# A first chunk from three batches in a chunked mLSTM with two dense blocks

## The chip, the cores and the metric

The kernel runs on one core of a Trainium2 chip. The metric is the device time of one execution in microseconds, as the median of several runs. The core's engines are TensorE (PE; weight loads are PEld), VectorE (DVE), ScalarE (ACT), GpSimd (POOL) and SyncE (SP), which issues the DMA transfers here.

## The reference, cut to what matters

An mLSTM over 4 batches, 8 heads, 768 positions and head width 40, then two dense blocks on its 3072 tokens of width 320.

```python
for t in range(S):                      # per batch and head
    m_new = max(f[t] + m, i[t])
    C = exp(f[t] + m - m_new) * C + exp(i[t] - m_new) * outer(v[t], k[t])
    n = exp(f[t] + m - m_new) * n + exp(i[t] - m_new) * k[t]
    y[t] = sigmoid(o[t]) * (C @ q[t]) / max(abs(n @ q[t]), 1)
h = x @ w_in                            # 320 -> 2048
x2 = (max(h, 0) + alpha * min(h, 0)) @ w_out
out = max(x2 @ w1, x2 @ w2, x2 @ w3) @ w4   # 320 -> 768 -> 320
```

## The kernel before

The 3072 tokens are 24 tiles of 128 positions, six to a batch, and 8 chunks of three tiles (`CHUNKS`, L35). Tile number i is position i // 6 of the batches and i % 6 within one, called (batch, place) here.

Attention handles a tile at a time. Within it a score matrix is made per head (q and k), multiplied by decays (`db`), and multiplied with v; the earlier tiles of the batch come in through the carried state `C`. So a tile that is not the first of its batch also has an inter step (q on C), and one that is not the last a state step (k and weighted v, added to C). In TensorE's queue the score matmuls read `q`, the pov matmuls `va,db`, the state matmuls `vw,kv`, the inter matmuls `C,q`. Tiles of batch 0 go through `attention32` (L855) in float32. The others go through `attention` (L928): q, k, v and the score matrix are split into two 16-bit parts under scales of their batch (`batch_scale`, L746). There the matmuls read `qs,ks`, `vh,ph` and `cs,qs`, and the split q and k go through a staging tile `hl` that `qk_parts` (L915) fills for three tiles at once. `finish` (L842) divides, applies the output gate, splits the row for 16-bit matmuls, and transposes it into `xT`, by TensorE for the first three tiles (`BY_DMA`), by DMA after.

The first dense block works on a chunk: 16 units `m1_unit` (L1052) of 8 matmuls on `wi`, then `m2_tile` on `wo`. The second follows `LAG` = 4 chunks later with `m3_unit` on `wq` and `m4_tile` on `wp`. These four groups are the backbone of TensorE's work. The weights come as 64-bit floats; `f64_to_f32` and `conv` turn them into two 16-bit parts under a scale from norms that TensorE computes (matmuls on `cv`, `qs`, `ks`, borrowed as buffers for the conversion). `w_in` needs a last common factor, for which VectorE makes `dg` and TensorE multiplies it (`dg,ones`).

`gates` (L1290) makes all gate terms in two pieces of positions: the first `GSPLIT` = 2 tiles of each batch, and the rest. Decays go to memory (`ddr`) and come back spread over the partitions (`decays`, L790).

The order of instructions on every engine is not that of the program text. `Sched` records each operation, estimates its cost, and a list planner decides the order, and for some operations the engine. Where it expects TensorE to be idle early, it puts in fills, matmuls of ones that go nowhere (L569). So a changed dependency or buffer changes the order everywhere. Almost every instruction has line L574, where the planned operations are issued. Buffers are rings (`Ring`, L613): `q` has one buffer (L673), `db` two (L678), and a ring may borrow others through `more`.

Of the kernel before, what the change touches and what calls it, by code (L numbers as in the profile page):

```python
# [22 lines left out]
CT = S // 128  # L23
# [13 lines left out]
NMAX = max(CHUNKS) * 128  # L37
GSPLIT = 2

# [91 lines left out]
class Sched:  # L131
# [429 lines left out]
    def issue(self, order):  # L561
        lead = int(self.LEAD / 213)
        for i in order:
            op = self.ops[i]
            e = self.engines[op.eng]
            if op.eng == "pe":
                k, n = self.fill.get(i, (0, 0))
                for _ in range(k + lead):
                    e.matmul(  # L569
                        out=self.tiles[n][:, 0:256], lhsT=self.warmth[:, 0:128], rhs=self.warmth, start=True, stop=True  # L570
                    )
                lead = 0
            for meth, kw in op.calls:
                getattr(e, meth)(**{k: v.on(v.bank.tile) if isinstance(v, View) else v for k, v in kw.items()})  # L574
# [11 lines left out]
def kernel(  # L586
# [44 lines left out]
    id16 = sbt("id16", [128, 128], F16)  # L631
    ones_ = sbt("ones", [128, 256], BF16)
    ones = ones_[:, 0:128]
    sc.warmth = ones_
    al = sbt("al", [128, KF])
# [64 lines left out]

    r_cv.more = [t.rearrange("p h t -> p (h t)").bitcast(I32) for t in r_qs.t + r_ks.t]


# [80 lines left out]
    def sigmoids(g):  # L784
        t = r_sig()
        sp.dma_start(out=t, in_=tok[3 * g:3 * g + 3, :, 3, :].rearrange("c p d -> p c d"))
        act.activation(out=t, in_=t, func=ACTF.Sigmoid)
        sig_t[g] = t
# [28 lines left out]

    def state(c, kv, vw, gm):

        pcv = half(bank("a"))  # L820
        sc.unit()
        for h in range(4):
            for hh in range(2):
                k = 4 * hh + h

                pe.matmul(
                    out=pcv[64 * hh:64 * hh + 64, h], lhsT=kv[:, 0, k * D:k * D + 64], rhs=vw[:, k], start=True, stop=True
                )
        sc.end()
        if c == 0:  # L830
            cn = carry["C"] = r_c()
            copy(cn, pcv)
        else:
            cn = carry["C"]
# [6 lines left out]

    def finish(i, num, least, xt, t0):  # L842

# [7 lines left out]
        dve.tensor_tensor(out=y, in0=num[:, :, 0:D], in1=bc(dn, [128, H, D]), op=ALU.mult)  # L851
        combine(y, y, sig_t[i // 3][:, i % 3].rearrange("p (h d) -> p h d", d=D), ALU.mult)
        to_xT(split_x(y.rearrange("p h d -> p (h d)"), rx[:, i:i + 1]), xt, t0, i >= BY_DMA)

    def attention32(i, xt, t0):  # L855

        b, c = divmod(i, CT)
        last = c == CT - 1
        if i % 3 == 0:
            sigmoids(i // 3)  # L860
        t = r_q()
# [20 lines left out]
        if c:  # L882
            cn = carry["C"]
            for hh in range(2):
# [12 lines left out]
        if not last:  # L897
            vw = r_vw()
            combine(vw, va, bc(gt[2].unsqueeze(2), [128, H, VA]), ALU.mult)
            state(c, kv, vw, gm)  # L900
        pov = per_head(bank("a"))
# [9 lines left out]
        else:  # L911
            copy(num, pov)
        finish(i, num, 1.0, xt, t0)

    def qk_parts(i):  # L915

        x = scl[:, i // CT]
        for s in range(2):
            t, hl = r_q(), r_hl()
            for u in range(3):  # L920
                sp.dma_start(out=t[40 * u:40 * u + 40], in_=qk[i + u, s])
            for hh in range(2):
                sl = slice(4 * hh, 4 * hh + 4)
                scaled(hl[0:120, 0, sl], t[0:120, sl], x[0:120, 3 + s:4 + s])
                rest(hl[0:120, 1, sl], t[0:120, sl], x[0:120, 3 + s:4 + s], hl[0:120, 0, sl])
            carry[s] = hl

    def attention(i, xt, t0):  # L928

        b, c = divmod(i, CT)  # L930
        last = c == CT - 1
        x = scl[:, b]
        if i % 3 == 0:
            sigmoids(i // 3)
            qk_parts(i)
        gt, db, gm = decays(i)
        qs, ks = r_qs(), r_ks()
        u = 40 * (i % 3)
        for dst, hl, parts in ((qs, carry[0], (0, 0, 1)), (ks, carry[1], (0, 1, 0))):
# [23 lines left out]
        num = r_num()  # L963
        if c:
            cs = carry["cs"]
            piv = per_head(bank("a"))
# [8 lines left out]
        if not last:  # L975
            vw = r_vw()
            combine(vw[:, :, 0:D], v, bc(gt[2].unsqueeze(2), [128, H, D]), ALU.mult)
            dve.tensor_scalar(out=vw[:, :, D], in0=gt[2], scalar1=x[:, 10:11], scalar2=None, op0=ALU.mult)
            cn = state(c, kv, vw, gm)
            cp = r_cp()  # L980
            scaled(cp[:, 0], cn, x[:, 9:10])
            rest(cp[:, 1], cn, x[:, 9:10], cp[:, 0])
            cs = carry["cs"] = r_cs()
            for hh in range(2):
                sp.dma_start(
                    out=cpd[i, :, :, 4 * hh:4 * hh + 4].rearrange("a d h v -> d a (h v)"),
                    in_=cp[64 * hh:64 * hh + 40].rearrange("p a h v -> p a (h v)"),
                )
            sp.dma_start(out=cs[0:80], in_=cpd[i].rearrange("a d h v -> (a d) h v"))
            sp.dma_start(out=cs[80:120], in_=cpd[i, 0])  # L990

        pov = per_head(bank("a"))
        sc.unit()
        for h in range(H):
            for n, (a, e) in enumerate(((0, 0), (0, 1), (1, 0))):
                pe.matmul(out=pov[:, h], lhsT=ph[:, a, h], rhs=vh[:, e, h], start=(n == 0), stop=(n == 2))
        sc.end()
# [5 lines left out]
        else:  # L1003
            copy(num, pov)
        finish(i, num, x[:, 7:8], xt, t0)

# [91 lines left out]
    def m3_unit(j, f):  # L1098
# [18 lines left out]
        combine(h2_t[:, f, 1, 0:n], v, h2_t[:, f, 0, 0:n], ALU.subtract)  # L1117

    def m4_tile(j, t):
        i = ROW0[j] + t  # L1120
# [12 lines left out]
        iv = r_iv()  # L1133
        if i % CT == 0:
            dve.tensor_tensor(out=scl[:, i // CT, 8:9], in0=scl[:, i // CT, 2:3], in1=kw, op=ALU.mult)
        dve.scalar_tensor_tensor(
            out=iv, in0=rx[:, i:i + 1], scalar=scl[:, i // CT, 8:9], in1=rx2[:, i:i + 1], op0=ALU.mult, op1=ALU.mult
        )
        ob = r_ob()
        scaled(ob, ps, iv)  # L1140
        sp.dma_start(out=out[i * 128:(i + 1) * 128, :], in_=ob)

# [147 lines left out]
    def gates():  # L1290
# [11 lines left out]
        for c0, c1 in ((0, GSPLIT), (GSPLIT, CT)):  # L1302
# [12 lines left out]
            )  # L1315
            for b in range(B):
                sp.dma_start(
# [31 lines left out]
    def attend(j):  # L1349
        for t in range(CHUNKS[j]):  # L1350
            i = ROW0[j] + t
            (attention if i >= CT else attention32)(i, xT[j % 2], 128 * t)
            b, c = divmod(i, CT)
            if c == 1 and 0 < b < B - 1:
# [36 lines left out]
    with tc.manual_schedule():  # L1391
        make_identity(nc, ident)
        nc.vector.tensor_copy(out=id16, in_=ident)
        nc.vector.memset(ones_, 1.0)
        for t in r_va.t:
# [67 lines left out]
```

## Time and profile before

| | |
|---|---|
| median of 3 runs | 720.55 us (719.22 to 721.73) |
| span of the profiled execution | 717.8 us |
| that execution's own time around the span | not given by the page |
| TensorE busy | 685.9 us, 96% |
| VectorE, ScalarE, GpSimd busy | 484.9, 415.8, 159.4 us |
| mean granted TensorE clock | 0.950 of 2.4 GHz |

The span goes from the first to the last instruction. Busy time of TensorE in the profile counts a matmul from its modelled start to its end, whatever share of the array it uses. A granted clock of 1.00 is 2.4 GHz, 0.50 is 1.2 GHz.

### The profile page before, as it was taken

How to read it: one execution, taken by the hardware profiler on the slowest of the kernel's cores; microseconds unless marked ns; L12 is line 12 of the kernel's file. 1: busy time of each engine (PE TensorE's matmuls, PEld its weight loads, DVE VectorE, ACT ScalarE, POOL GpSimd, SP SyncE). 2: the span in 40 equal slices, each digit the busy share in tenths (PEclk: the TensorE clock that was granted, in tenths of full speed). 3: DMA queues.
4: the chain of work that ended last, by engine and by line, in shares of the span. 5: the costliest groups of instructions: out<-in, count | busy, mean ns of one | idle time of the engine just before them, and what ended most of it. 6: DMA issues, size and time to landing. Idle time of an engine off the chain costs nothing.

```text
span 717.8 us, 14674 instructions
## 1 busy us (share of the span) xinstructions
PE 685.9 (96%) x5299; PEld 464.1 (65%) x5299; DVE 484.9 (68%) x1256; ACT 415.8 (58%) x983; POOL 159.4 (22%) x193
## 2 busy tenths in 40 slices
PE   4789999999899999999999999999999999999998
PEld 3678766666566666666666666666766676666665
DVE  7676879999799899899579963786265223242332
ACT  4667769899799889887467662662253122222222
POOL 1221242044251362166014310330031000000000
PEclk8555799999999999999999999999999999999999
DMA  8865476565794656863443362122201110002000
GB/s 251 280 189 188 154 225 190 165 194 161 230 292 123 203 168 182 244 190 92 104 137 119 122 136 88 45 64 38 59 19 33 28 50 12 28 1 61 8 21 27
DMA packets 82802, 88.33 MB, mean 123 GB/s; under 512 B 38754, under 2 KB 66218, under 8 KB 82730
## 3 DMA queue, kind: packets, MB, share of 16 engines
q1 hardware_dynamic: 82730, 87.40, 42.2%
q8 instruction: 41, 0.67, 0.4%
q14 instruction: 31, 0.25, 0.1%
HBM read 60.83 MB, written 8.75 MB: 97 GB/s over the span
## 4 chain that ended last, share of the span: by engine, by line
PE 59%; DVE 2%; issue 0%; DMA 0%; SPq 0%; ACT 0%; ACTq 0%
PE bank L574 59%; DMA cs<-cpd 0%; SPq L574 0%; DVE wq L574 0%; DVE h L574 0%; DVE hl L574 0%; DVE vw L574 0%; DVE g L574 0%; DVE cp L574 0%; ACT db L574 0%; DVE y L574 0%; DVE gf L574 0%; DVE xs L574 0%; DVE cv L574 0%; ACT ob L574 0%
## 5 line engine op out<-in xcount | busy, mean ns | idle before, releaser
L574 PE MATMUL bank<-xT,wi 128*128 128x384 f16 x1024 | 177.1, 328 | 0.2 <-DVE gf L574 0.2
L574 PE MATMUL bank<-wo,g 128*128 128x320 f16 x1152 | 165.3, 299 | 0.6 <-DVE g L574 0.6
L574 PEld LDWEIGHTS <-wq 128*128 128x128 f16 x1152 | 110.9, 98 | 71.2 <-issue 0.5
L574 PEld LDWEIGHTS <-g 128*128 128x128 f16 x1152 | 110.9, 98 | 44.8 <-DVE g L574 0.9
L574 PEld LDWEIGHTS <-wi 128*128 128x128 f16 x1024 | 98.8, 98 | 62.3 <-issue 2.0
L574 PE MATMUL bank<-x2T,wq 128*128 128x384 f16 x720 | 123.1, 326 | 0.4 <-DVE gf L574 0.4
L574 POOL TENSOR_TENSOR g<-gf,g 128x384 f16<-128x384 f32 x63 | 60.6, 964 | 174.1 <-DVE g L574 95.3
L574 DVE TENSOR_TENSOR mv<-bank,mv 128x384 f32<-128x384 f32 x96 | 52.9, 551 | 60.4 <-PE bank L574 59.5
L574 DVE SCALAR_TENSOR_TENSOR gf<-d,al,bank 128x384 f32<-128x384 f32 x128 | 76.5, 603 | 9.9 <-ACT d L574 9.1
L574 ACT ACTIVATE h<-mv 128x384 f16<-128x384 f32 x47 | 24.5, 521 | 94.1 <-DVE mv L574 94.1
L574 ACT ACTIVATE d<-bank 128x384 f32<-128x384 f32 x128 | 61.1, 479 | 20.1 <-PE bank L574 18.8
L574 PE MATMUL bank<-xT,wq 128*128 128x384 f16 x432 | 70.7, 326 | 0.0
L574 ACT ACTIVATE db<-db,gtok 128x128 f32<-128x128 f32 x192 | 63.4, 390 | 9.1 <-POOL db L574 8.9
L574 ACT ACTIVATE g<-gf 128x384 f16<-128x384 f32 x104 | 53.7, 519 | 20.0 <-DVE gf L574 19.7
L574 PE MATMUL bank<-wp,h 128*128 128x320 f16 x432 | 61.0, 299 | 0.0
L574 PEld LDWEIGHTS <-h 128*128 128x128 f16 x432 | 42.1, 98 | 16.7
L574 POOL TENSOR_TENSOR h<-mv,h 128x384 f16<-128x384 f32 x14 | 13.8, 983 | 161.1 <-ACT h L574 161.0
L574 DVE TENSOR_TENSOR g<-gf,g 128x384 f16<-128x384 f32 x65 | 39.2, 610 | 11.3 <-ACT g L574 11.1
L574 POOL TENSOR_SCALAR_AFFINE_SELECT db<-db 128x512 f32<-128x512 f32 x48 | 36.7, 784 | 40.5 <-ACT gm L574 25.8
L574 DVE TENSOR_TENSOR db<-bank,db 128x512 f32<-128x512 f32 x48 | 31.8, 682 | 7.3 <-PE bank L574 2.0
L574 DVE TENSOR_SCALAR sx<-sx 128x1 int32<-128x1 int32 x48 | 7.0, 146 | 40.5 <-ACT xs L574 40.2
L574 ACT ACTIVATE xs<-bank 128x320 f16<-128x320 f32 x24 | 10.3, 429 | 37.1 <-PE bank L574 36.5
(170 smaller groups left out, 890.3 us busy)
## 6 DMA issues: line engine op xcount, KB each, us to landing
db<-ddr SPq DMA_DIRECT2D x24, 512.0 KB
raw<-tok SPq DMA_DIRECT2D x18, 480.0 KB
kv<-tok SPq DMA_DIRECT2D x24, 320.0 KB
q<-qk SPq DMA_DIRECT2D x36, 160.0 KB
raw<-w_out SPq DMA_DIRECT2D x16, 320.0 KB
raw<-w SPq DMA_DIRECT2D x9, 512.0 KB
qs<-hl SPq DMA_DIRECT2D x54, 80.0 KB
ks<-hl SPq DMA_DIRECT2D x54, 80.0 KB
```

What stands on the lines that cost most here:

```text
L574: getattr(e, meth)(**{k: v.on(v.bank.tile) if isinstance(v, View) else v for k, v in kw.items()})
```

## The change

The first chunk is now the first tile of batches 0, 1 and 2. After it come the remaining tiles in batch order: (0,1) to (0,5), (1,1) to (1,5), (2,1) to (2,5), then all six of batch 3 (`ORDER`). The three tiles of the first chunk and those of batch 0 go through `attention32` (`whole`), so eight tiles are float32, before six. The states of batches 1 and 2 that this leaves are kept (a second `C` buffer, and a borrowed `wp` buffer for batch 1) and split into 16-bit parts only when the second tile of the batch is reached (`state_parts`). `qk_parts` takes two tiles at once for places 1 and 2 of batches 1 and 2 (`GROUPS`). The gates are first made for 128 positions of each batch, then for 640. For the first tiles `q` borrows the `ph` buffer and one `hl` buffer, and `db` the other `hl`. The ones tile for fills is half as wide, and the fill reads it twice. The diff, cut:

```diff
-GSPLIT = 2
+GSPLIT = 1
+ORDER = [(b, 0) for b in range(B - 1)] + [(b, c) for b in range(B) for c in range(b < B - 1, CT)]
+GROUPS = {(b, c): n for b in range(B) for c, n in (((1, 2), (3, 3)) if b < B - 1 else ((0, 3), (3, 3)))}
+def whole(p):
+    b, c = ORDER[p]
+    return b == 0 or (c == 0 and b < B - 1)
...
-                        out=self.tiles[n][:, 0:256], lhsT=self.warmth[:, 0:128], rhs=self.warmth, start=True, stop=True
+                        out=self.tiles[n][:, 0:256].rearrange("p (a k) -> p a k", a=2), lhsT=self.warmth,
+                        rhs=self.warmth.unsqueeze(1).to_broadcast([128, 2, 128]), start=True, stop=True,
...
-    r_c = Ring("C", 1, [128, 4, VA])
+    r_c = Ring("C", 2, [128, 4, VA])
...
         if c == 0:
-            cn = carry["C"] = r_c()
+            cn = wp_s[KF2][:, 0:4 * VA].rearrange("p (h v) -> p h v", v=VA) if b == 1 else r_c()
+            carry["C", b] = cn
...
-    def qk_parts(i):
-        x = scl[:, i // CT]
+    def qk_parts(i, n):
+        x, r = scl[:, i // CT], slice(0, 40 * n)
...
+            if c == 1 and b < B - 1:
+                cn = carry["C", b]
+                dve.tensor_scalar(
+                    out=cn[:, :, D], in0=cn[:, :, D], scalar1=x[:, 10:11], scalar2=None, op0=ALU.mult
+                )
+                state_parts(i - 1, cn, x)
...
-            for b in range(B):
+            if c1 == 1:
+                sp.dma_start(out=ddr[0].rearrange("b c (h t) -> (b c h) t", t=128), in_=delta[:, t])
+            for b in range(B if c1 > 1 else 0):
...
             i = ROW0[j] + t
-            (attention if i >= CT else attention32)(i, xT[j % 2], 128 * t)
-            b, c = divmod(i, CT)
+            if i == 0:
+                r_q.more = [as_q(r_ph.t[0]), as_q(r_hl.t[0])]
+                r_db.more = [as_q(r_hl.t[1])]
+            elif i == 3:
+                r_q.more, r_db.more = r_q.more[:1], []
+            elif i == 8:
+                r_q.more = []
+            (attention32 if whole(i) else attention)(i, xT[j % 2], 128 * t)
+            b, c = ORDER[i]
```

The planner makes new orders from this. Three places follow; `ph` and `hl` in a score or inter matmul are borrowed q buffers, `hl` also a borrowed decay buffer. On TensorE, from the matmul on `dg` on, there stood before the inter step of the third tile, its pov and its state:

```order
L574 MATMUL bank_69<-dg_190,ones 128x4
L574 MATMUL bank_68<-C_168,q_149 128x41 x4
L574 MATMUL bank_64<-C_168,q_149 128x41 x4
L574 MATMUL bank_65<-va_161,db_158 128x41 x8
L574 MATMUL bank_67<-vw_164,kv_156 64x41 x8
```

and now the score step of the fourth tile (two banks in turn, four each) and the pov of the third:

```order
L586 MATMUL bank_67<-dg_191,ones 128x4
L586 MATMUL bank_66<-ph_165 128x128
L586 MATMUL bank_68<-ph_165 128x128
...
L586 MATMUL bank_64<-va_161,hl_151 128x41 x8
L586 LDWEIGHTS xs_145
```

The third tile has no inter step any more. On TensorE again, just ahead of the first backbone matmul (on `wi`), there stood the second half of the fifth tile's inter step, three norms, and 15 fills:

```order
L574 MATMUL bank_70<-C_168,q_149 128x41 x4
L574 LDWEIGHTS cv_137
L574 MATMUL bank_66<-cv_137 128x128
...
L569 MATMUL bank_67<-ones 128x256
...
L574 LDWEIGHTS wi_88
L574 MATMUL bank_67<-xT_130,wi_88 128x384
```

and now fills, and then the pov and the state of the fifth tile among three norms:

```order
L580 MATMUL bank_67<-ones 128x256
L586 MATMUL bank_67<-va_161,db_158 128x41 x8
L586 LDWEIGHTS cv_137
L586 MATMUL bank_63<-cv_137 128x128
L586 MATMUL bank_68<-vw_164,kv_156 64x41 x8
...
L586 LDWEIGHTS wi_88
L586 MATMUL bank_64<-xT_130,wi_88 128x384
```

Counted from the start, TensorE's queue holds ahead of the first wi matmul 48 score, 40 pov, 40 state and 16 inter matmuls and 58 fills; before they were 40, 32, 32, 32 and 60. In the whole program 64 score and 64 pov matmuls in float32 stand against 48 and 48, 128 on qs,ks against 144, 384 on vh,ph against 432; the state (160) and float32 inter (40) matmuls and the backbone are equal. On SP, from the first decay load to the last pieces of w_in, there stood before

```order
L574 DMA db_158<-ddr_84 128x1024
L574 DMA ddr_85<-g_128 8x4x128
L574 DMA db_159<-ddr_84 128x1024
L574 DMA q_149<-qk 40x512
L574 DMA raw_134<-w_in 128x1024
L574 DMA raw_135<-w_in 64x512 x2
L574 DMA raw_133<-w_in 128x1024
L574 DMA q_149<-qk 40x512 x2
L574 DMA kv_156<-tok 128x2x320
L574 DMA al<-alpha 128x16
L574 DMA raw_134<-w_in 128x1024
```

and now

```order
L586 DMA db_158<-ddr_84 128x1024
L586 DMA db_159<-ddr_84 128x1024
L586 DMA kv_157<-tok 128x2x320
L586 DMA raw_134<-w_in 128x1024
L586 DMA raw_135<-w_in 64x512 x2
L586 DMA raw_133<-w_in 128x1024
L586 DMA hl_151<-ddr_84 128x1024
L586 DMA hl_150<-qk 40x512
L586 DMA al<-alpha 128x16
L586 DMA hl_150<-qk 40x512 x3
L586 DMA kv_156<-tok 128x2x320
L586 DMA raw_134<-w_in 128x1024
```

A third decay load (`hl_151`) and the third tile's q and k (`hl_150`) now come before the last pieces of w_in.

## Rows read from the trace of the kernel before

**Rows 1.** The page: busy time by engine, and the granted clock in 40 slices.

```profile
PE 685.9 (96%) x5299; PEld 464.1 (65%) x5299; DVE 484.9 (68%) x1256; ACT 415.8 (58%) x983; POOL 159.4 (22%) x193
PEclk8555799999999999999999999999999999999999
```

**Rows 2.** The chain of waits that ended last: start us, us, what.

```profile
324.48 390.08 PE bank L574 x2869
```

**Rows 3.** Busy time by stretch: PE, PEld, DVE, ACT, POOL, clock, DMA share, GB/s.

```profile
48.00:76.00 28.00, 28.00 (x176) 23.23 (x175) 18.65 (x58) 23.17 (x51) 4.48 (x7) 0.50 0.64 196
76.00:82.00 6.00, 6.00 (x52) 5.03 (x52) 4.97 (x9) 3.01 (x7) 1.89 (x3) 0.78 0.42 126
130.00:300.00 170.00, 162.34 (x1490) 110.91 (x1489) 157.13 (x430) 152.51 (x377) 58.20 (x62) 1.00 0.68 194
```

**Rows 4.** TensorE in order of time, to the first backbone matmul: start us, us, group.

```profile
26.58 3.63 PE L574 MATMUL bank<-va,db 128*128 128x41 f32 x16 [2.75 <-DVE db L574]
...
47.56 0.16 PE L574 MATMUL bank<-dg,ones 128*128 128x4 bf16 x1 [2.37 <-DVE dg L574]
47.66 2.81 PE L574 MATMUL bank<-C,q 40*128 40x41 f32 x16
...
53.96 1.08 PE L574 MATMUL bank<-vw,kv 128*64 128x41 f32 x16
...
55.92 2.08 PE L574 MATMUL bank<-q 40*128 40x128 f32 x16
...
58.79 1.93 PE L574 MATMUL bank<-C,q 40*128 40x41 f32 x8
...
62.79 1.76 PE L574 MATMUL bank<-cv 128*128 128x128 bf16 x9
...
70.96 1.89 PE L569 MATMUL bank<-ones 128*128 128x256 bf16 x8
...
81.95 1.96 PE L574 MATMUL bank<-xT,wi 128*128 128x384 f16 x8
```

**Rows 5.** What TensorE waited for from 82 us on: in total, times, longest.

```profile
PE bank L574 <- DMA ks<-hl: 3.0, 2, 2.3
...
PE bank L569 <- DVE gf L574: 0.4, 1, 0.4
```

**Rows 6.** Busy time by 5 us stretch, columns as in rows 3.

```profile
30.00:35.00 5.00, 5.00 (x31) 4.65 (x32) 3.63 (x13) 3.69 (x11) 0.46 (x1) 0.50 0.98 325
...
95.00:100.00 5.00, 5.00 (x27) 3.39 (x27) 3.15 (x6) 0.40 (x1) 2.02 (x3) 0.66 1.11 325
```

**Rows 7.** ScalarE and SP in order of time: the last piece of w_in.

```profile
39.74 0.41 ACT L574 ACTIVATE qs<-raw 128x256 f32<-128x256 f32 x1
...
31.03 1.11 SPq L574 DMA_DIRECT2D raw<-w_in  x2
```

**Rows 8.** TensorE in order of time after the start.

```profile
85.35 1.47 PE L574 MATMUL bank<-xT,wi 128*128 128x384 f16 x8
...
88.07 1.93 PE L574 MATMUL bank<-va,db 128*128 128x41 f32 x16
...
89.94 0.68 PE L574 MATMUL bank<-vw,kv 128*64 128x41 f32 x16
...
93.52 1.16 PE L574 MATMUL bank<-q 40*128 40x128 f32 x16
...
94.78 1.08 PE L574 MATMUL bank<-C,q 40*128 40x41 f32 x8
...
95.95 1.37 PE L574 MATMUL bank<-C,q 40*128 40x41 f32 x8
...
97.44 2.72 PE L574 MATMUL bank<-xT,wi 128*128 128x384 f16 x8
```

**Rows 9.** TensorE's groups of instructions, shapes apart: count, busy us, mean ns.

```profile
L574 PE MATMUL bank<-vh,ph 128*128 128x41 f16 x432 | 13.8, 180 | 0.0
L574 PE MATMUL bank<-qs,ks 120*128 120x128 f16 x144 | 12.2, 219 | 5.2 <-DMA ks<-hl 3.0 <-DMA cs<-cpd 1.4 <-DMA cpd<-cp 0.8
```

More of the change, by code (lines that the diff above doesn't have):

```diff
@@ L631 @@
     id16 = sbt("id16", [128, 128], F16)
[L632 to L634 removed]
+    ones = sbt("ones", [128, 128], BF16)
+    sc.warmth = ones
     al = sbt("al", [128, KF])
@@ L785, in sigmoids @@
         t = r_sig()
-        sp.dma_start(out=t, in_=tok[3 * g:3 * g + 3, :, 3, :].rearrange("c p d -> p c d"))
+        at = [b * CT + c for b, c in ORDER[3 * g:3 * g + 3]]
+        if g == 0:
+            rows = tok.rearrange("(b c) p k d -> b c p k d", c=CT)[0:3, 0, :, 3, :]
+            sp.dma_start(out=t, in_=rows.rearrange("c p d -> p c d"))
+        else:
+            u = 0
+            while u < 3:
+                v = u + 1
+                while v < 3 and at[v] == at[v - 1] + 1:
+                    v += 1
+                sp.dma_start(out=t[:, u:v], in_=tok[at[u]:at[v - 1] + 1, :, 3, :].rearrange("c p d -> p c d"))
+                u = v
         act.activation(out=t, in_=t, func=ACTF.Sigmoid)
@@ L816, in per_head, with state @@
         return b[:, 0:H * VA].rearrange("p (h v) -> p h v", v=VA)
-    def state(c, kv, vw, gm):
+    def state(b, c, kv, vw, gm):
         pcv = half(bank("a"))
@@ L840, in half, with finish @@
         return b[:, 0:4 * VA].rearrange("p (h v) -> p h v", v=VA)
-    def finish(i, num, least, xt, t0):
+    def finish(n, num, least, xt, t0):
         dn = r_dn()
@@ L899, in attention32 @@
             combine(vw, va, bc(gt[2].unsqueeze(2), [128, H, VA]), ALU.mult)
-            state(c, kv, vw, gm)
+            state(b, c, kv, vw, gm)
         pov = per_head(bank("a"))
@@ L912, in attention32, with state_parts @@
             copy(num, pov)
-        finish(i, num, 1.0, xt, t0)
-    def qk_parts(i):
-        x = scl[:, i // CT]
+        finish(n, num, 1.0, xt, t0)
+    def state_parts(i, cn, x):
+        cp = r_cp()
+        scaled(cp[:, 0], cn, x[:, 9:10])
+        rest(cp[:, 1], cn, x[:, 9:10], cp[:, 0])
+        cs = carry["cs"] = r_cs()
+        for hh in range(2):
+            sp.dma_start(
+                out=cpd[i, :, :, 4 * hh:4 * hh + 4].rearrange("a d h v -> d a (h v)"),
+                in_=cp[64 * hh:64 * hh + 40].rearrange("p a h v -> p a (h v)"),
+            )
+        sp.dma_start(out=cs[0:80], in_=cpd[i].rearrange("a d h v -> (a d) h v"))
+        sp.dma_start(out=cs[80:120], in_=cpd[i, 0])
+    def qk_parts(i, n):
+        x, r = scl[:, i // CT], slice(0, 40 * n)
         for s in range(2):
             t, hl = r_q(), r_hl()
-            for u in range(3):
+            for u in range(n):
                 sp.dma_start(out=t[40 * u:40 * u + 40], in_=qk[i + u, s])
@@ L923, in qk_parts, with attention @@
                 sl = slice(4 * hh, 4 * hh + 4)
-                scaled(hl[0:120, 0, sl], t[0:120, sl], x[0:120, 3 + s:4 + s])
-                rest(hl[0:120, 1, sl], t[0:120, sl], x[0:120, 3 + s:4 + s], hl[0:120, 0, sl])
+                scaled(hl[r, 0, sl], t[r, sl], x[r, 3 + s:4 + s])
+                rest(hl[r, 1, sl], t[r, sl], x[r, 3 + s:4 + s], hl[r, 0, sl])
             carry[s] = hl
-    def attention(i, xt, t0):
-        b, c = divmod(i, CT)
+        carry["first"] = i
+    def attention(n, xt, t0):
+        b, c = ORDER[n]
+        i = b * CT + c
         last = c == CT - 1
         x = scl[:, b]
-        if i % 3 == 0:
-            sigmoids(i // 3)
-            qk_parts(i)
+        if n % 3 == 0:
+            sigmoids(n // 3)
+        if (b, c) in GROUPS:
+            qk_parts(i, GROUPS[b, c])
         gt, db, gm = decays(i)
         qs, ks = r_qs(), r_ks()
-        u = 40 * (i % 3)
+        u = 40 * (i - carry["first"])
         for dst, hl, parts in ((qs, carry[0], (0, 0, 1)), (ks, carry[1], (0, 1, 0))):
@@ L978, in attention @@
             dve.tensor_scalar(out=vw[:, :, D], in0=gt[2], scalar1=x[:, 10:11], scalar2=None, op0=ALU.mult)
[L979 to L990, printed above, removed]
+            cn = state(b, c, kv, vw, gm)
+            state_parts(i, cn, x)
         pov = per_head(bank("a"))
@@ L994, in attention @@
         for h in range(H):
-            for n, (a, e) in enumerate(((0, 0), (0, 1), (1, 0))):
-                pe.matmul(out=pov[:, h], lhsT=ph[:, a, h], rhs=vh[:, e, h], start=(n == 0), stop=(n == 2))
+            for k, (a, e) in enumerate(((0, 0), (0, 1), (1, 0))):
+                pe.matmul(out=pov[:, h], lhsT=ph[:, a, h], rhs=vh[:, e, h], start=(k == 0), stop=(k == 2))
         sc.end()
@@ L1004, in attention @@
             copy(num, pov)
-        finish(i, num, x[:, 7:8], xt, t0)
+        finish(n, num, x[:, 7:8], xt, t0)
     def split_x(src, r):
@@ L1133, in m4_tile @@
         iv = r_iv()
[L1134 to L1135 removed]
+        b, c = ORDER[i]
+        u = 0 if whole(i) else b
+        if u not in out_scales:
+            out_scales.add(u)
+            dve.tensor_tensor(out=scl[:, u, 8:9], in0=scl[:, u, 2:3], in1=kw, op=ALU.mult)
         dve.scalar_tensor_tensor(
[L1137 removed]
+            out=iv, in0=rx[:, i:i + 1], scalar=scl[:, u, 8:9], in1=rx2[:, i:i + 1], op0=ALU.mult, op1=ALU.mult
         )
@@ L1140, in m4_tile @@
         scaled(ob, ps, iv)
-        sp.dma_start(out=out[i * 128:(i + 1) * 128, :], in_=ob)
+        row = (b * CT + c) * 128
+        sp.dma_start(out=out[row:row + 128, :], in_=ob)
     def raw_load(parts, n):
```

24 lines of the change are left out of this document (15 added, 9 removed).

## The prediction

> **What bounds the kernel now.** I read the page first: TensorE is busy for 96% of the span, and its granted clock is at half (digit 5, the 1.2 GHz level) only in a few of the first slices [rows 1]. The chain of waits that ended last then shows who sets the end: one unbroken run of 2869 matmuls from 324 us on [rows 2]. So whatever the change does, it must do it through TensorE's queue, by less work in it, by an earlier start, or by fewer waits. The stretches [rows 3] split the span into three stages. From 48 to 76 us TensorE has no idle time, but all of it at 0.50. From 130 to 300 us it is busy 162.34 of 170 us at 1.00, with VectorE almost as full (157.13). The backbone, the matmuls on wi, wo, wq and wp, starts at 81.95 us [rows 4]. Ahead of it TensorE does small float32 attention matmuls, norms of the weights and fills. The one wait of size there is for dg, 2.37 us, at 47.56 us, where VectorE makes it late [rows 4]. The waits after the start are ten groups from 3.0 to 0.4 us, 12.1 us together [rows 5].
>
> I therefore cost the change by TensorE's queue in its two orders, and count an attention step in its units: per tile 8 score matmuls, 8 on va (pov), 8 on vw (state), 8 on C (inter, two halves of 4). A float32 unit is two records in the trace.
>
> **Part 1: up to dg.** Tiles 1 and 2 of the first chunk lose their inter step and no longer hang on C. But TensorE waits for dg there anyway, and dg follows the last w_in norm. The SP order puts the first decay load where it was, behind the same w_in piece and the same number of transfers, so the first pov at 26.58 us [rows 4] stays. What is moved ahead of the last w_in pieces is a third decay load (512 KB) and four q pieces of 80 KB: 0.83 MB, at the 325 GB/s of that stretch [rows 6] 2.6 us. ScalarE turns the last piece only 8.7 us after its issue (31.03 to 39.74 us, [rows 7]), so the delay has cover; without that cover dg comes 2.6 us later. At best dg comes earlier by its wait, 2.4 us, since VectorE has four num operations fewer. I take 0 between -2.4 and +2.6, because both orders hold the same w_in operations ahead of dg.
>
> **Part 2: from dg to the first backbone matmul, at the 1.2 GHz level.** Counted in the two orders, this piece gains one score step (8 matmuls), one pov and one state, and loses one inter step and two fills; norms (33) and transposes (15) stay. Prices at half clock [rows 4]: score 2.08, pov 3.63, state 1.08, fill 1.89/8 = 0.24; an inter step costs 2.81 with its halves together and 2 x 1.93 = 3.86 with them apart. That gives 2.08 + 3.63 + 1.08 - 3.86 - 0.47 = +2.5 us, or +3.5 with the halves together; I take **+3.0**. So the first chunk's independence buys no earlier start: the pov and the state of the fifth tile now stand ahead of the first wi matmul. Before, 15 fills stood there. This assumes the same 3.4 us at full clock ahead of the start as now (the 76 to 82 us stretch is at 0.78, [rows 3]).
>
> **Part 3: from there to the end, at 2.4 GHz.** Two tiles change from the 16-bit to the float32 path. Left to do after the start: one pov more (+1.93), one score step more (+1.16), one state less (-0.68), two inter steps more (2 x (1.08 + 1.37) = +4.90), all at the full-clock rows [rows 8]; 16 matmuls qs,ks fewer at 12.2/144 = 0.085 (-1.36) and 48 matmuls vh,ph fewer at 13.8/432 = 0.032 (-1.53) [rows 9]. Sum **+4.4**. The backbone counts (1024, 1152, 1152, 432) are equal.
>
> **Part 4: waits after the start.** The first 16-bit tile now comes ninth instead of seventh, so the staging transfers have more time: ks<-hl 3.0, cs<-cpd 1.4 and cpd<-cp 0.8 are 5.2 us [rows 9]. The later tiles' transfers remain, so I take half, **-2.6**, between 0 and -5.2.
>
> **At nothing.** VectorE gains 8 instructions net, ScalarE loses 2, GpSimd 16 and SP 9; all run beside TensorE. The cover is thin between 130 and 300 us: 12.9 us of VectorE's 170 are free [rows 3], and if that goes, TensorE waits for gf and g. The gates do the same columns as 128 + 640 instead of 256 + 512. The fills keep 256 columns. The column D scaling of C and the state parts are the same steps later; two extra small VectorE operations are well under 1 us.
>
> **Sum.** +0 + 3.0 + 4.4 - 2.6 = +4.8 us on the profiled span of 717.8 us: 722.6 us. The page gives no time around the span; the median of the runs is 2.75 us above it, so I forecast **725.4 us**. A difference under 0.3% (2.2 us) can't be told from no change.
>
> **The clock, a rule against the trace.** From 48 to 76 us TensorE shows 28.00 busy of 28 us and the clock stays at 0.50 [rows 3]; it rises after 8 and then more fills from 70.96 us on [rows 4], falls again in part of 95 to 100 us [rows 6], and there 8 backbone matmuls took 2.72 us instead of 1.47 [rows 8]. The Trainium skill, TensorE: Matmul & The Clock Gate, section "What's actually happening", says "the default state is throttled, and activity releases the throttle". By that alone the rise should have come long before 76 us; the trace does not agree as far as busy time in the profile is activity, so small float32 matmuls seem not to weigh like fills (a guess). It is one of the rivals because the change shifts where fills stand.
>
> **The rivals.**
> - *The clock is released earlier (faster).* The new order has 8 fills in a row at its first group, where the old one has 3. From there to the first wi matmul stand about 28 us of half-clock work (two pov, one score step, three states, two inter halves, 18 norms at 1.76/9, 32 fills, transposes, [rows 4]). If all of it ran at full clock, less the 3.4 us that the forecast has already (6.8 at half), 21/2 = 10.6 us go: 714.8 us. It decides from a granted clock of 1.00 before the state of the third tile. For it: the longer group. Against it: the old norms and fills at 62 to 66 us did not raise it. Chance 0.2.
> - *The waits pay it back (no change).* All staging waits go (-5.2) and half of the other 6.9 us of waits (-3.4), since the stage from 82 us on holds two tiles less of splitting work on VectorE and ScalarE: 717.8 + 7.4 - 8.6 = 716.6, plus 2.75: 719.4 us. With the order hardly moving the start (TensorE row 368 against 366), that is also the case that the change does not do what it says. Against it: VectorE's total does not fall. Chance 0.2.
> - *The start slips (much slower).* dg comes 2.6 us late behind the extra transfers, and no full-clock stretch lies ahead of the first wi matmul (+3.4), so its first 16 matmuls run at half clock too (2 x 1.25): 725.4 + 8.5 = 734 us. Chance 0.15.
>
> **Numbers.** The forecast has 0.45; alone it spans 722.8 (staging waits gone) to 730 (no full-clock stretch ahead of the start). Faster is the first rival, 0.2; same the second, 0.2; slower the forecast and the last rival, 0.6. The range goes from 714 to 734: half of the outer rivals' chance lies outside.
>
> **What would show it.** Right: the pov of the fifth tile ahead of the first wi matmul; that matmul at 82 to 88 us; C matmuls of two more tiles after it; TensorE's busy time up by some 5 us; ks<-hl waits shorter. Wrong: a first wi matmul well under 80 us, the clock at 1.00 before 70 us, or PE waits after the start well off 7 to 12 us.

## The result, and the profile after

The changed kernel takes **723.37 us** (median of 11 runs, 721.19 to 730.4), the kernel before 720.55 (median of 11, 716.42 to 723.45). The ratio is **1.0055**, 95% interval 1.0032 to 1.0078: slower by half a per cent, 2.8 us by the medians, where 4.8 were forecast. Runs that took over 1.5% more than the fastest of their kernel are left out of this ratio and of those below: nine of the twelve of E8, the profiled one among them, one of E14 and one of the kernel before. The profiled execution took 723.83 us, with a span of 722.0, 4.2 us above that of before. So the sums below are of 4.2 us, the difference of two single executions.

The page of the changed kernel, busy time and granted clock, answers to [rows 1]:

```profile
PE 688.9 (95%) x5298; PEld 467.0 (65%) x5298; DVE 490.0 (68%) x1264; ACT 414.5 (57%) x981; POOL 139.3 (19%) x177
PEclk8555699999999999999999999999999999999999
```

TensorE's busy time is up by 3.0 us. Busy time by stretch, columns as in [rows 3]:

```profile
48.00:76.00 28.00, 28.00 (x184) 23.42 (x184) 19.12 (x62) 20.85 (x42) 1.67 (x3) 0.50 0.61 190
76.00:82.00 6.00, 6.00 (x29) 4.76 (x28) 4.49 (x14) 5.44 (x14) 1.24 (x2) 0.50 0.41 132
...
84.00:88.00 4.00, 4.00 (x44) 3.48 (x43) 1.05 (x3) 1.38 (x5) 0.61 (x1) 0.90 0.12 35
130.00:300.00 170.00, 163.31 (x1447) 111.94 (x1446) 157.46 (x427) 145.39 (x359) 52.52 (x62) 1.00 0.63 179
```

From 76 to 82 us the clock was 0.78 before and is 0.50 now: the half-clock stretch lasts to about 84.8 us (0.90 from 84 to 88 us) instead of 76, and then the clock stays full, where before it fell again twice. TensorE in order of time, as in [rows 4, 8]:

```profile
28.48 3.64 PE L586 MATMUL bank<-va,db 128*128 128x41 f32 x16 [4.72 <-DVE db L586]
...
48.06 0.16 PE L586 MATMUL bank<-dg,ones 128*128 128x4 bf16 x1
...
63.20 1.91 PE L580 MATMUL bank<-ones 128*128 128x256 bf16 x8
...
66.14 3.58 PE L586 MATMUL bank<-va,db 128*128 128x41 f32 x16
...
69.84 2.08 PE L586 MATMUL bank<-ph 40*128 40x128 f32 x16
...
74.84 1.92 PE L580 MATMUL bank<-ones 128*128 128x256 bf16 x8
...
81.14 1.68 PE L580 MATMUL bank<-ones 128*128 128x256 bf16 x7
...
83.13 1.70 PE L580 MATMUL bank<-ones 128*128 128x256 bf16 x7
84.62 1.97 PE L586 MATMUL bank<-va,db 128*128 128x41 f32 x16
...
87.27 2.76 PE L586 MATMUL bank<-xT,wi 128*128 128x384 f16 x16
```

The first pov is 1.9 us later, dg 0.5 us, and the first wi matmul 5.3 us (87.27 against 81.95), with the fifth tile's pov right ahead of it. What TensorE waited for from 82 us on (in total, times, longest), as in [rows 5]:

```profile
PE bank L586 <- DVE gf L586: 2.8, 4, 1.4
PE bank L586 <- DVE C L586: 1.8, 1, 1.8
PE bank L580 <- DVE gf L586: 1.4, 1, 1.4
PE bank L586 <- DVE wq L586: 1.0, 1, 1.0
```

With three small groups these are 8.0 us, against 12.1. The waits for transfers (ks<-hl, cs<-cpd, cpd<-cp) are gone whole; VectorE's gf has become the longest.

### The profile page after: what moved, and what is told of

Same layout as the page of the kernel before. It is cut to its first block, busy times and chain, and to the rows that moved or that the text cites. A ratio compares the mean times of both kernels' runs of the same rounds, so it can differ in the third digit from the quotient of the medians.

```text
span 722.0 us, 14642 instructions
## 1 busy us (share of the span) xinstructions
PE 688.9 (95%) x5298; PEld 467.0 (65%) x5298; DVE 490.0 (68%) x1264; ACT 414.5 (57%) x981; POOL 139.3 (19%) x177
## 4 chain that ended last, share of the span: by engine, by line
PE 77%; DVE 7%; DMA 6%; ACT 6%; issue 3%; SPq 1%; POOL 0%; ACTq 0%; POOLq 0%; DVEq 0%
PE bank L586 76%; DMA raw<-w_in 2%; DMA hl<-ddr 1%; DVE wq L586 1%; DVE g L586 1%; ACT g L586 1%; PE bank L580 1%; ACT d L586 1%; DMA cpd<-cp 1%; DVE xs L586 1%; ACT db L586 1%; DMA raw<-w 1%; DVE gf L586 1%; DMA cs<-cpd 1%; ACT raw L586 1%
## 5 line engine op out<-in xcount | busy, mean ns | idle before, releaser
L586 POOL TENSOR_TENSOR g<-gf,g 128x384 f16<-128x384 f32 x59 | 55.0, 935 | 192.2 <-DVE g L586 94.1
L586 ACT ACTIVATE db<-db,gtok 128x128 f32<-128x128 f32 x184 | 61.4, 391 | 5.5 <-POOL db L586 5.2
L586 DVE TENSOR_TENSOR g<-gf,g 128x384 f16<-128x384 f32 x69 | 42.9, 631 | 8.7 <-ACT g L586 8.1
L586 POOL TENSOR_SCALAR_AFFINE_SELECT db<-db 128x512 f32<-128x512 f32 x46 | 31.4, 701 | 89.3 <-ACT gm L586 66.9
L586 POOL TENSOR_TENSOR h<-mv,h 128x384 f16<-128x384 f32 x12 | 11.3, 938 | 165.7 <-ACT h L586 161.5
L586 DVE TENSOR_TENSOR h<-mv,h 128x384 f16<-128x384 f32 x36 | 20.3, 566 | 17.1 <-ACT h L586 17.1
L586 ACT ACTIVATE mv<-bank 128x384 f32<-128x384 f32 x40 | 19.4, 486 | 19.4 <-PE bank L586 16.7
```

## A balance for all kernels

To compare plans I split each span in three, by stretches of one us: **idle** is the stretch less TensorE's busy time; **half clock** is busy time times (1 - granted clock), what the lower level cost; **work** is the rest, matmul time as if at 2.4 GHz. The second figure of half clock is its part in falls of the clock after it had become full behind the first wi matmul. Each line is one profiled execution and the ratio is that of the runs; the numbers 5 and 13 are not used. "Old" and "new" name the tiles (six or eight in float32).

Two cautions. The runs came in four groups on several chips, each group beside runs of the kernel before (medians 720.55 beside the changed kernel, 721.32 beside E1 to E4, 721.37 for E6 to E9, 722.14 for E10 to E14), so medians of different groups compare only to 1 or 2 us, and the ratios are the fairer measure. And a profiled execution can lie some us off the median of its kernel: E14's took 718.5 us (median 722.63), E12's 721.03 (717.83), E3's 720.48 (717.79).

```
kernel                      median  ratio to before, 95%      span   work  idle (after 48 us)  half clock (late)  first wi
before                      720.55                            717.8  656.8  31.9 (15.3)         29.1 (1.7)        81.95
after                       723.37  1.0055 [1.0032, 1.0078]   722.0  660.7  33.1 (12.0)         28.1 (0.0)        87.27
E1  after, no fills         721.42  1.0013 [0.9987, 1.0040]   721.4  657.0  32.0 (12.7)         32.4 (3.4)        82.63
E2  before, no fills        719.22  0.9986 [0.9959, 1.0014]   716.9  652.2  35.8 (17.6)         28.9 (0.0)        79.01
E3  after, gates as before  717.79  0.9963 [0.9933, 0.9992]   718.7  661.4  32.1 (12.5)         25.3 (4.4)        70.69
E4  new tiles, old order    721.15  1.0008 [0.9981, 1.0035]   719.0  656.9  26.7 ( 8.6)         35.4 (1.7)        88.49
E6  before, other costs     730.59  1.0125 [1.0083, 1.0167]   726.8  660.2  43.8 (25.8)         22.8 (1.7)        81.72
E7  after, other costs      717.24  0.9949 [0.9922, 0.9976]   715.2  661.0  29.9 (12.1)         24.3 (1.7)        68.64
E9  after, forced start     712.63  0.9873 [0.9835, 0.9910]   710.4  663.9  27.3 (11.0)         19.2 (0.0)        73.53
E10 before, forced start    725.87  1.0057 [1.0025, 1.0088]   723.6  655.9  38.0 (19.4)         29.8 (3.4)        77.64
E11 E9, no fills            717.53  0.9926 [0.9894, 0.9959]   714.7  655.9  32.1 (13.4)         26.7 (1.7)        74.56
E12 E9, gates as before     717.83  0.9944 [0.9918, 0.9969]   719.0  660.3  30.1 (10.1)         28.6 (0.0)        84.29
E14 E9, fourth tile too     722.63  1.0010 [0.9978, 1.0042]   716.7  662.2  32.4 (12.9)         22.1 (3.2)        70.69
```

For the change itself: +3.9 work, +1.2 idle (+4.6 before 48 us, -3.3 behind), -1.0 half clock, +4.2 together (rounded).

## The experiments

The theory: the changed kernel is slower because two more float32 tiles put more work into TensorE's queue, part of it at half clock ahead of the first wi matmul. Rivals: the split of the gates and its extra load; the fills; the order of the tiles; or just another plan.

**E1 and E2: no fills.** Both kernels keep their order, and all fills but the 26 at the very start go.

```
-                for _ in range(k + lead):
+                for _ in range(lead):
```

> The changed kernel without the 32 fill matmuls that stand between the gate work and the first wi matmul (and the 3 after it); every other instruction keeps its place. They fill no result, so the output is the same. Theory (the queue of TensorE sets the start): the fills of that stretch, 8 + 1 + 8 + 1 + 7 + 7 in six groups of 1.91, 0.41, 1.92, 0.41, 1.68 and 1.70 us, are 8.0 us of work ahead of the first wi matmul, and the granted clock rises at about the same time without them: first wi at 79 to 82 us instead of 87.27, run 3 to 7 us below the changed kernel, 716 to 720 us. Rival 1 (the fills buy the clock): without them the half clock lasts past the start, PE waits take the fills' place, and the run is within 2 us of the changed kernel, 721 to 725. Rival 2 (the half clock stays for tens of us): slower, 727 or more.

> The kernel before without its 34 fill matmuls ahead of the first wi matmul and the 2 after it (0.84 + 1.89 + 1.05 + 1.06 + 3.02 = 7.9 us ahead); nothing else moves. Theory: what the fills cost they cost in both kernels, so it falls by the same 3 to 7 us as the changed kernel does without them, to 714 to 718 us, and the distance between the two kernels stays 1 to 4 us. Rival (the distance between the kernels is the place where the fills landed, 3.02 us of them at full clock before and none in the changed kernel): the distance closes to under 1 us once both have none.

The changed kernel came to 721.42 us, the kernel before to 719.22, neither told apart from before. Against their own versions with fills that is 2.0 and 1.3 us less by the medians, 3.0 and 1.0 by the ratios, so at best the low end of the theory's 3 to 7. TensorE of E1 in order of time, and two stretches of it:

```profile
82.63 4.70 PE L586 MATMUL bank<-xT,wi 128*128 128x384 f16 x16
```

```profile
84.00:86.00 2.00, 2.00 (x8) 0.96 (x7) 2.00 (x9) 0.57 (x2) 0.00 (x0) 0.50 0.93 266
86.00:90.00 4.00, 4.00 (x32) 3.07 (x31) 2.80 (x9) 1.68 (x5) 0.36 (x1) 0.93 0.47 151
```

The start is 4.6 us earlier, but the wi matmuls now run at half clock themselves: 16 take 4.70 us instead of 2.76. The balance against the changed kernel is -3.7 work, -1.1 idle, +4.3 half clock. Of the 4.3, 3.4 are two later falls of the clock in this one execution, and 0.8 come from the start, where the clock is full from 86.5 us instead of 84.8. So rival 1 of E1 has the mechanism, the half clock lasts past the start, but how much of their cost the fills bought back in clock is open between 0.8 and 4.3 us. In E2 it is -4.6 work and +3.9 idle. The distance between the kernels is 2.2 us by the medians without fills and 2.8 with them, so the fills do not seem to be what separates the two.

**E3: the split of the gates undone.**

```
-GSPLIT = 1
+GSPLIT = 2
```

> The changed kernel with its gates made for 256 positions first, as before (the split of the gates undone, all else kept, the order planned anew). Theory: the split moves only the first pov, by 1 to 2 us, and what follows depends on TensorE's queue, so the first wi matmul stays within 3 us of 87.27 and the run within 3 us of 723.4. Rival (the split gates and the third load of decays ahead of the w_in loads are the loss): first wi at 80 to 83 us, run at 718 to 720. Other rival (the split is the gain that holds the loss down): first pov at 31 us or later, first wi past 90, run at 727 or more.

At 717.79 us it is faster than before, and 5.6 us below the changed kernel: my theory missed. But the mechanism is not the one that the rival named. TensorE in order of time:

```profile
29.36 3.63 PE L586 MATMUL bank<-va,db 128*128 128x41 f32 x16 [5.91 <-DVE db L586]
...
70.69 2.77 PE L586 MATMUL bank<-xT,wi 128*128 128x384 f16 x8
...
84.24 1.87 PE L586 MATMUL bank<-va,db 128*128 128x41 f32 x16
```

The first pov is even later than with the split. The new plan put the first wi matmuls at 70.69 us and the fifth tile behind them, its pov at 84.24 us, and the half clock cost 25.3 us instead of 28.1 (20.9 without the later falls).

**E4: new tiles in the old order**, gates as before; eight float32 tiles remain.

```
-ORDER = [(b, 0) for b in range(B - 1)] + [(b, c) for b in range(B) for c in range(b < B - 1, CT)]
+ORDER = [(b, c) for b in range(B) for c in range(CT)]
-        if g == 0:
+        if g < 0:
```

> The changed kernel with the tiles in the old order (all six of batch 0, then batch 1) and the gates' split undone, but with the first tiles of batches 1 and 2 still on the float32 path, so that path alone differs from before, apart from the buffers. Theory (the content of TensorE's queue): two more float32 tiles are 2 x (1.95 + 1.16 - 0.78 - 0.68) = +3.3 us of matmuls at full clock, and the start stays near that of before: first wi at 80 to 84 us, run at 722 to 725. Rival 1 (the order does it): without the new order the run is that of before, 720 to 721. Rival 2 (the float32 path relieves the loads of the parts, so waits fall by what its matmuls add): 718 to 721 with PE busy 3 us up and waits on DMA gone.

721.15 us, not told apart from before. The first wi matmul comes at 88.49 us, later than in any other kernel, and the half clock costs most of all (35.4), but idle time is the least (8.6 after 48 us). That is a third way, a mixture: the float32 path saves waits (Rival 2), and the late start eats that. It is also 3.4 us above E3, which differs from it in the order of tiles alone (the intervals just overlap), so no loss by the order is seen there.

**E6 and E7: other costs for the planner.** Its float32 matmuls were too cheap against [rows 4, 8]: pov takes 1.93 us for 8 at 2.4 GHz, the plan had 0.88.

```
-                dur = max(busy / pair + 3.5, (110.0 if wide else 60.0) / (1.5 if pair == 2 else 1))
+                dur = (145.0 if n > 64 else 270.0) if pair == 2 else (244.0 if wide else 84.0)
```

> The kernel before, planned with other costs for the small float32 matmuls, taken from the trace at 2.4 GHz: 244 ns for one of pov (1.95 us for 8), 270 for one of the carried part (1.08 for 4), 145 for one of the scores (1.16 for 8), 84 for one of the state; the plan had 110, 73, 110 and 72. Nothing computed changes; the planner finds TensorE fuller and puts 24 fills in place of 34 ahead of the first wi matmul and seven rows of the state and scores of the fifth tile behind it. Theory (the granted clock rises 3 to 5 us after the wide matmuls begin, be they fills or wi, and each us earlier is half a us of matmul time): first wi at 75 to 80 us, run 717 to 720.5 us, against 721.3. Rival (the plan before was as good as plans get here, other orders scatter around it): 721 to 725.

> The changed kernel planned with the same four costs for float32 matmuls; gates still first made for 128 positions. The plan now puts three pov ahead of the first wi matmul, where it had five, and 19 fills, where it had 32. Theory (what delays the changed kernel is the stretch of small float32 matmuls ahead of the wi matmuls, at half clock because the wide matmuls come late): first wi at 70 to 77 us, the granted clock at 1.00 from 74 to 81, the loss to the half clock down by 2 to 5 us, run 717 to 720.5. Rival (the split of the gates is the loss, since undoing it gave 717.8): still 722 to 725, whatever the order.

E7 came out as the theory had it, with an even earlier start: first wi matmul at 68.64 us (70 to 77 expected), half clock down by 3.8 us, 717.24 us. Its split of the gates is that of the changed kernel, so the split by itself is not the loss. E6 missed widely: 730.59 us with the first wi matmul at 81.72 us (75 to 80 expected), though its half clock cost fell by 6.3 us. What TensorE of E6 waited for from 82 us on:

```profile
PE bank L574 <- DMA xT<-xT: 2.8, 1, 2.8
PE bank L574 <- DVE sx L574: 2.4, 2, 1.7
PE bank L574 <- DVE vw L574: 1.7, 2, 1.4
PE bank L574 <- ACT mv L574: 1.6, 1, 1.6
```

With twelve smaller groups these are 17.5 us, against 12.1 before, and all idle time after 48 us is 25.8 us, against 15.3: more than the clock gave. Why this plan makes the later tiles late, no run tells.

**E8: the split alone, in the kernel before.**

```
-GSPLIT = 2
+GSPLIT = 1
```

> The kernel before with its gates first made for 128 positions, nothing else of the change. The second tile of batch 0 now needs the gates of the remaining five tiles. Theory (the split alone is worth a us or two, the rest is where the plan puts the wide matmuls): first pov 2 to 4 us earlier or later than 26.58, pov of the second tile later than 37, first wi within 4 us of 81.95, run 719 to 723. Rival (the split is the loss): 723.5 to 727. Other rival (the split is a gain, which the changed kernel spends elsewhere): under 718.5.

The ratio is 0.9984 (interval 0.9939 to 1.0028) and rests on three runs of 718.4 to 722.3 us: not told apart from before, and too few runs to speak for or against the split. Its profile shows an order that missed the theory: the first pov at 26.94 us and the first wi matmul at 88.46.

**E9: the fifth tile behind the first wi matmuls.** One dependency more, planned anew:

```
         sc.end()
+        carry.setdefault("wi", len(sc.ops) - 1)
...
         sc.end()
+        if n == 4:
+            sc.after(carry["wi"])
```

(The first in m1_unit, the second behind the score matmuls of attention32.)

> The changed kernel with one order forced: the scores of its fifth tile (the second of the second chunk) come after the first group of wi matmuls, so that its pov no longer stands ahead of them; planned anew with the old costs, 47 fills ahead of the first wi matmul in place of 32. Theory (early wide matmuls, be they fills or wi, raise the granted clock early, and the fifth tile's 8 us of float32 work at half clock is then done at full clock): first wi at 74 to 80 us, clock at 1.00 by 80, run 717.5 to 721. Rival (the fills take the place of what was moved and the total stays): 722 to 725. Other rival (the split of the gates is the loss): 722 to 725 too, but with the clock at 1.00 by 80.

**712.63 us**, ratio 0.9873: 1.3% faster than before, better than forecast, with the first wi matmul at 73.53 us (74 to 80 expected), and the best kernel here. TensorE in order of time, then two stretches:

```profile
57.16 1.27 PE L580 MATMUL bank<-ones 128*128 128x256 bf16 x5
...
59.91 2.76 PE L580 MATMUL bank<-ones 128*128 128x256 bf16 x12
...
62.91 1.16 PE L586 MATMUL bank<-ph 40*128 40x128 f32 x16
64.00 1.98 PE L586 MATMUL bank<-va,db 128*128 128x41 f32 x16
...
73.53 1.46 PE L586 MATMUL bank<-xT,wi 128*128 128x384 f16 x8
...
86.42 1.93 PE L586 MATMUL bank<-va,db 128*128 128x41 f32 x16
```

```profile
56.00:62.00 6.00, 6.00 (x32) 3.75 (x32) 6.00 (x21) 4.26 (x10) 0.00 (x0) 0.50 0.63 163
62.00:66.00 4.00, 4.00 (x44) 3.52 (x41) 1.36 (x5) 1.09 (x3) 0.00 (x0) 0.93 0.71 252
```

From 56 to 62.6 us TensorE does 20 fills with only bf16 norms among them, and the clock is full from there: the sixth tile's scores (on `ph`) take 1.16 us and the fourth tile's pov 1.98, where the changed kernel has 2.08 (69.84 us) and 3.58 (66.14). The balance against the changed kernel is -8.9 half clock, -5.8 idle (4.8 of it before 48 us), +3.2 work. Its profile has the highest mean clock of its six runs, 0.964 of 0.957 to 0.964.

**E10: the same order forced in the kernel before** (the same lines, with i in place of n).

> The kernel before with the order forced that gave the changed kernel 712.6: the scores of the fifth tile come after the first group of wi matmuls; planned anew, 15 fills ahead of that group where before had 34. Theory (the place of the fifth tile, not the change's tile order, is worth the 10 us): the same treatment takes 4 to 10 us off the kernel before too, 711 to 717 us, and the change is again worth plus or minus 3 us. Rival (the forced order pays only with the changed kernel's order of tiles, whose fifth tile needs no carried state ahead of the others): 718 to 723 us.

725.87 us: the theory missed, and so did the rival, which said no worse than 723. Only 15 fills stand ahead of the start, the half clock costs as much as before (29.8, of which 3.4 in later falls), and the waits are longer. What TensorE of E10 waited for from 82 us on:

```profile
PE bank L574 <- DVE gf L574: 3.9, 6, 1.7
PE bank L574 <- DMA ks<-hl: 3.3, 2, 2.3
PE bank L574 <- DMA xT<-xT: 2.7, 1, 2.7
```

So an early start is no gain by itself: it paid in E9, where the clock rose early and the idle time did not grow, and not in E10, where the idle time grew by 6.1 us.

**E11: E9 without its fills**, as E1.

> The version with the forced start (712.6 us) without any of its fills but the 26 at the very start; every other instruction keeps its place. 47 fills ahead of the first wi matmul go, some 5 us of matmuls at full clock and up to twice that at half clock. Theory A (the fills raise the granted clock from 63 us on, and that is the gain): without them the clock reaches 1.00 only 3 to 5 us after the first wi matmul, at 70 us or later, the loss to the half clock grows by 3 to 6 us, idle time takes part of the fills' place, and the run is 713 to 719. Theory B (the order alone is the gain, the fills only fill): 708 to 712.5, first wi at 65 to 69 us.

717.53 us, 4.9 us above E9 by the medians and 3.8 by the ratios, whose intervals just overlap: theory A. TensorE in order of time, then two stretches:

```profile
63.54 3.63 PE L586 MATMUL bank<-va,db 128*128 128x41 f32 x16
...
74.56 2.56 PE L586 MATMUL bank<-xT,wi 128*128 128x384 f16 x8
```

```profile
62.00:66.00 4.00, 4.00 (x28) 3.78 (x26) 2.68 (x11) 2.25 (x5) 0.00 (x0) 0.50 0.88 283
66.00:74.00 8.00, 8.00 (x65) 6.64 (x64) 6.10 (x16) 5.45 (x9) 1.10 (x2) 0.50 0.54 185
```

The first wi matmul stays within 1.1 us of its place without 47 fills, since everything ahead of it runs at half clock now. The half clock costs 7.5 us more (5.8 without a later fall), idle time 4.8 more, and 8.0 us of work are saved. The order is worth 3.9 us by the medians and 6.3 by the ratios without fills (E1 to E11), 10.7 and 13.1 with them (the changed kernel to E9): fills that cost the changed kernel 2 to 3 us net gain 4 to 5 in this order.

**E12: E9 with the gates as before.**

> The version with the forced start (712.6 us) with the gates made for 256 positions first, as before. With the start forced, the split of the gates is compared in two kernels whose fifth tile has the same place; unforced, undoing it took the changed kernel from 723.4 to 717.8. Theory (undoing the split only happened to give a plan with the wi matmuls early): here it is worth under 3 us either way, 710 to 716. Rival (the split itself costs 4 to 6 us): 706 to 709. Other rival (the split itself gains): 717 or more.

717.83 us, 5.2 above E9: the third case, the split gains. Unforced, undoing it had *gained* 5.6 us (E3). In E12 the fills come late, in order of time:

```profile
78.57 2.74 PE L580 MATMUL bank<-ones 128*128 128x256 bf16 x12
...
82.59 1.91 PE L580 MATMUL bank<-ones 128*128 128x256 bf16 x8
84.29 2.08 PE L586 MATMUL bank<-xT,wi 128*128 128x384 f16 x8
```

The clock is full from about 85.5 us only. A sign that turns with the plan is not the split's own effect; its own share stays open.

**E14: E9 with the fourth tile moved too** (`if n in (3, 4)`).

> The version with the forced start, one tile further: the scores of the fourth tile (the first of the second chunk) as well as of the fifth come after the first group of wi matmuls; 39 fills stand between the gate work and it. Theory (each tile of float32 work taken from the half clock to full clock gains 2 to 4 us, as long as fills or wi keep TensorE busy with wide matmuls): first wi at 64 to 72 us, run 708 to 712. Rival (there is nothing left to gain, since the clock was already full at 63 us and the fourth tile's pov already took 1.98 us): 712 to 716. Other rival (the second chunk's tiles come too late, and m1 of the second chunk waits for them): 717 or more, with new waits between 100 and 300 us.

722.63 us, worse than E9 by 10 us: the other rival is nearest. Its profile is of its fastest run (718.5), so the rows show 6 of the 10 us. What TensorE waited for from 82 us on:

```profile
PE bank L586 <- DVE cv L586: 2.8, 2, 2.1
PE bank L586 <- DMA db<-ddr: 2.1, 1, 2.1
```

The wait for a tile's decays is new (at 199 us). The clock rises 3 us later than in E9 (at 65.5 us), yet up to the start the half clock costs no more (18.9 us against 19.2); two later falls cost 3.2 us, and idle time is 5.1 us more.

## Why the prediction was right, and where not

The number held, 723.37 against 725.4 with a range of 714 to 734, and so did its direction. By its own steps, against the spans:

- **Part 1** (0, between -2.4 and +2.6): +0.5. The first pov did not stay, it came 1.9 us later with a wait of 4.72 us for db, but dg hid that, as the step said.
- **Part 2** (+3.0): from dg to the first wi matmul 39.2 us against 34.4, **+4.8**. The mechanism was right, two terms were mis-sized. By kinds, the rows of that stretch summed: score +2.6 (forecast 2.08), pov +2.1 (3.63), state +0.7 (1.08), inter -1.35 (-2.8 to -3.9), fills +0.2 (-0.5), norms and transposes +0.1. These rows overlap each other in both kernels, so they sum to 4.2 of the 4.8. The inter step was the main miss: before, one of the three ran partly at full clock, and both that remain have their halves apart, 4 x 1.93 us. The fifth pov was cheaper, since it ran at full clock (1.97). The assumption of 3.4 us at full clock ahead of the start was near: 84.8 to 87.27 us, 2.5.
- **Part 3** (+4.4): TensorE is busy for 622.8 us from the first wi matmul on, against 620.5, **+2.3**. The counts were right. Left out was that before lost 2.2 us to the half clock behind its start, as around 97 us [rows 6, 8], and the changed kernel nothing: 4.4 - 2.2 = 2.2. That this fits so well is partly luck: the inter half of 1.37 us [rows 8], priced as a full-clock row, spans the fall at 96.6 us. At 1.08 us, as the other half, the step comes to +3.8, and 0.7 us of the 2.3 stay unexplained.
- **Part 4** (-2.6): idle time behind the start fell from 15.4 to 11.9 us, **-3.4**. By the groups of waits it is -4.1: all 5.2 us of staging waits went, where I took half, and 1.1 us came back with gf and C. The kernels of the table with the old tiles (before, E2, E6, E10) wait 3.5 to 6.2 us for transfers after 82 us, those with the new ones 0 to 2.1, and E4, with the old order, not at all. So the saving seems to come with the float32 tiles and not with their order, though E8's profile, with the old tiles, has only 2.0 us.
- **Sum**: 0.5 + 4.8 + 2.3 - 3.4 = +4.2, against +4.8. That it came so near is in part luck: Part 2 was 1.8 us too low and Part 3 2.1 too high, and the two cancel. The step from span to median was too large for the changed kernel: 723.37 lies 1.4 us above its span, not 2.75. The difference of the medians is thus smaller than that of the profiles.

The rivals: *the clock is released earlier* was wrong for the changed kernel. The 8 fills in a row at 63.20 us changed nothing, and neither did those at 74.84; the clock stayed at 0.50 to 84.8 us. But its mechanism is real, and E9 shows it: full clock from 62.6 us, 8.9 us less half-clock cost, where the rival reckoned 10.6. *The waits pay it back* came half true: the staging waits went, the rest did not. *The start slips* went the right way by its first term only, +0.5 us in place of 2.6.

What the prediction did not see is that the plan around the start weighs more than the change. Seven plans with the new tiles (all but E1 and E11, which only leave out fills) lie from 712.6 to 723.4 us, and the changed kernel's is the slowest of them; three with the old tiles (before, E6, E10; E8 left out) lie from 720.5 to 730.6. With the old tiles TensorE idles 15 to 26 us after 48 us, with the new ones 9 to 13. The change thus trades about 4 us of float32 work for as many us of waits or more; what it ends up as depends on how long TensorE stays at half clock, 19 to 35 us of cost in these plans, and on the idle time that the plan leaves: E14 and E6 have little half clock (22.1 and 22.8 us) and are slow all the same. The work is the weaker half of that trade: by the balance, with some 0.12 us taken off for each fill, the kernels with the old tiles have 649 to 653 us, those with the new ones 652 to 655, and one order with and without fills differs by 1.6 us already (E9 and E11).

The Trainium skill says (TensorE: Matmul & The Clock Gate, section "What's actually happening") that activity releases the throttle. The changed kernel speaks against that again if busy time is taken for activity: 34.00 of 34 us busy from 48 to 82 us at 0.50. E9 and E11 agree with it in that the rise came with what TensorE did: with its fills this order is at full clock from 62.6 us, without them it stays at 0.50 until 76.8 us, in the first wi matmuls.

Still open: the split's own effect (E3 against E12, with E8 resting on three runs), why E10 gets so few fills, and what the new tiles by themselves are worth, since every version was planned anew and no run holds the plan fixed while it changes the tiles.

## What to carry to other kernels

When an engine is full throughout, split its span into work, idle time and the cost of the lower clock, for each plan; a change that moves work between them shows there even where the total hardly moves. Compare several plans on both sides before crediting a change with a few us: here one forced dependency was worth 10.7 us by the medians, nearly four times the change. Where a stretch of small float32 matmuls runs at 1.2 GHz, try putting part of it behind fills and wide matmuls: that paid in E9, and did not where the fills stood scattered (E1, E2) or where the work put off made later stages wait (E10, E14).

## What the runs showed of the hardware

- What TensorE did before its clock rose: in E9 20 fills from 57.16 us with only bf16 norms among them, the rise at 62.6 us; in E11 part of the first 8 wi matmuls from 74.56 us, the rise at 76.8 us. In the changed kernel eight fills in a row at 63.20 and at 74.84 us, between norms and float32 groups, were followed by no rise until 84.8 us, and in E12 20 fills from 78.57 us, with 0.8 us idle between the first 12 and the last 8, by none until 85.5 us. So a count of fills alone does not tell these cases apart.
- The clock also fell while TensorE had no idle time: in the kernel before at 79.5 us (busy 6.00 of the 6 us from 76 on, [rows 3]) in the first of 15 fills that followed float32 score and inter matmuls and three norms, and at 96.6 us (5.00 of the 5 us from 95 on, [rows 6]) within an inter group.
- The mean granted clock of one kernel differs from run to run. Of 35 runs of the kernel before on one chip, the 11 with a mean clock of 0.954 or more took 719.4 us on average, the 9 with 0.947 or less 723.9. That is more than the change is worth. The Trainium skill says (TensorE: Matmul & The Clock Gate, section "What's actually happening") that one kernel has different numbers of slow matmuls from run to run. These runs agree as far as a lower mean clock stands for more of them.
- A float32 matmul of 128x41 on full weights costs 0.24 us at 2.4 GHz (1.93 / 8) and 0.45 at 1.2 GHz (3.63 / 8); one of 128x384 in f16 costs 0.18 (1.46 / 8). So 41 columns in float32 are dearer than 384 in f16.
